# An S4D convolution block with a top-1 mixture of experts: gathers among the experts' work, one load per quarter, drains per expert, a new order

## The chip, the cores and the metric

The kernel runs on one core of a Trainium2 chip. The metric is the device time of one execution in microseconds; the number compared is the median of several timed runs. Besides these there is one profiled execution, from which all rows below come. The core has five engines with a queue each: TensorE (PE; its weight loads are shown as PEld), VectorE (DVE), ScalarE (ACT), GpSimd (POOL), and SyncE (SP), which mostly issues DMAs. ScalarE and GpSimd issue DMAs too.

## The reference

Input `u` is 2048 rows of 512 channels, there are 8 experts with a hidden size of 1792.

```python
# A: S4D convolution over the sequence, N=128 states per channel
dt = exp(log_dt); A = -exp(log_A_real) + 1j * A_imag; C = (C_real + 1j * C_imag) * dt[:, None]
P = exp((A * dt[:, None])[:, :, None] * pos)
K = 2.0 * einsum("dn,dnl->dl", C, P).real
y = irfft(rfft(u_t, 2 * L) * rfft(K, 2 * L), 2 * L)[:, :, :L]   # causal convolution
A_out = y^T + u * D_skip
# B: one expert for each row
gates = softmax(xt @ wg); expert = argmax(gates)
B_out = g * gelu(xt @ w1[expert]) @ w2[expert]                  # g: the normalized gate, 1 for one expert
# whole
h  = x + A(layernorm(x))
h2 = h + B(layernorm(h))
```

The kernel computes every expert for up to a fixed number of rows (288 for the fullest, 232 for the emptiest, `CAPS`), in three parts of up to 96 rows, and treats rows beyond that in a loop at the end which runs as often as there are such rows.

## The kernel before

**Front.** Up to about 310 us the kernel normalizes `u`, transforms it (`u_s1`, `u_ev1`, `u_s2`, `u_ev2`, `spread` copies into `uw`), stores it to a scratch in HBM (`ud`), and builds the convolution's spectra from the state-space parameters (`t_...`). Then the convolution is made for four blocks of 128 channels (`conv`): a block has eight parts `rc`, each of which is loaded, transformed (`c_s2`), multiplied with the spectrum (`c_z`), transformed back in a first step (`c_ia`, L785 and L786), copied from PSUM to a tile `ys` (`c_ys`, L790) and stored to the scratch `yd` (`c_yst`, L793). Once the eight parts of a block are in `yd`, four quarters `q` of it are loaded in another arrangement (`c_y1`, L810) and go through the second step (`c_ib`, L838); the residual is added and the result `h` stored as `hd` in HBM (`r_st`, `r_hd`, L1058). `h` is transposed on PE, copied to tiles `ht` (`r_ev`, L1047) and multiplied with the gate weights (`r_lg`, L1054).

`ys` and `ht` share one pool tag with two buffers. For the last block the tiles of the quarters lie where the experts' weights will be, and each quarter is loaded in four pieces: rows up to 96 of 128 when the first six parts are stored (`c_y3`, two DMAs on SP), the remaining 32 after all eight (`c_y3s` on SP, `c_y3a` on ScalarE's queue).

**Routing.** From the logits VectorE finds each row's expert, its place among that expert's rows, and lists of row numbers: `gi0` for expert 0 and then `gi` for the others. The gate factors are written to HBM as a column `cwd` (`cw_scratch` in the profile).

**Experts.** For each expert `e` and part `k`, GpSimd gathers rows of `h` with their mean and deviation by an indirect DMA (`m_ga`, tile `rows`, 96x516) and the gate factors of these rows with another (`m_gc`, tile `cwt`, 96x1; L1305 is the helper's line for both). VectorE normalizes them, PE transposes, and each float32 matmul is made from three products of high and low parts (`xh`, `xl`; `h`, `l` of the weights: L1400 to L1402, L1423 to L1425). Weights come in slices of 512 KB by SP (`m_w1` in tiles `r1`, `m_w2` in tiles `r2`); ScalarE makes their high part (`m_h`, L1387), VectorE their low part (`m_l`, L1391). At the expert's end VectorE forms gate factor times result plus residual (`m_o`, tile `ot`, L1440) and GpSimd scatters it to the output by an indirect DMA (`m_sc`, L1298). `m_dr` is a drain on GpSimd's queue (L1458), once, behind all 24 scatters. `o_a` and the following prepare the loop over the remaining rows.

**What sets the order.** No task is issued where it is written. `at(t, engine, us, function, ...)` registers it with what it reads and writes; `_Plan.order` then places the tasks one after the other: on each engine, of those that can start within 0.1 us of the earliest, the one with the lowest number in the table `PRI` goes first. `ON` says for tasks that ScalarE or VectorE can do (engine "AV") which does each instance (A or V); where it has a dot the planner takes the one that can start first. `SW` is a penalty for a ScalarE task that needs another activation table. Planned durations are in the `at` calls; a DMA's result counts as there 0.9 us (SP) or 2.2 us (GpSimd) after the issue ends. Buffers are planned as rings (`RINGS`): a tile waits until the users of its slot are placed. The engines then run their queues in this order, held only by semaphores.

Of the kernel before, what the change touches and what calls it, by code (L numbers as in the profile page):

```python
# [22 lines left out]
KR = 3  # L23
# [4 lines left out]
YS = 96  # L28
# [4 lines left out]
def _constants():  # L33
# [11 lines left out]
    co, si = co.transpose(2, 1, 0) / L, si.transpose(2, 1, 0) / L  # L45
# [40 lines left out]
def _dram(ap, dims, off=0):  # L86
# [11 lines left out]
SW = 0  # L98
ON = {
    'p_ev': 'AAAA',  # L100
    'u_norm': 'VVVVAVAAVAVVVVVV',
    'u_ev1': 'AAAAAAAAAAAAAAVAVAAVVVVAAVAVAAVA',
    'u_ev2': 'AAAAAAAAAAAAAAAAVVVVVVVAAAAAAVAA',
    't_vc': 'AAAAAAVAAVAAAAAA',
    't_kt': 'AAAAVAAAAAAAAAAA',
    'c_ev1': 'AAAAAAAAAAAAAAVVAAAAAAVAAAVAAAAA',
    'c_ys': 'AVAAAAAAAAAVAAAAAAAAAAAAAAAAVVVA',
    'c_out': 'AAAAAAAA',
    'r_ev': 'AAAAAAAAAAVAAAAA',
    'r_cb': 'V',  # L110
    'r_c8': 'A',
    'm_xh': 'AAV',
    'm_gh': 'VVA',
}
PRI = {
    'l_wg': [19.9],
    'r_sw': [35.7],
    'r_swe': [43],
    'l_dt': [2],
    'l_x': [16.5, 3.4, 11.7, 6.8],  # L120
    'l_raw': [2.6, 10.9, 15.8, 10.2],
    'l_s1': [15.1],
    'l_m2': [25.5],
    'l_rest': [22.5],
    'p_dt': [3.7],
    'p_exp': [5.7],
    'p_scale': [6.8, 15.8, 21.4, 26.1],
    'p_tr': [7.9, 17.8, 22.4, 27.2],
    'p_ev': [9.6, 20.1, 29.7, 44.6],
    'u_stats': [22.1, 7.8, 16.6, 11.8],  # L130
    'u_mean': [29.4, 16.9],
    'u_dev': [31.7, 20.6],
    'u_var': [32.7, 21.6],
    'u_std': [34.4, 28.3],
    'u_rstd': [35, 28.8],
    'u_norm': [42, 43.1, 39, 37, 41.5, 38, 43, 39.9, 41, 38.4, 40, 36, 29.7, 30.7, 33.4, 32.4],
# [8 lines left out]
    'u_st': [70.1, 74.4, 78.7, 83, 89.1, 93.4, 97.7, 101.9, 112.4, 117.1, 121.4, 125.7, 131.1, 135.4, 139.7, 143.9],  # L145
    'open_main': [147.2],
    'm_load': [151.4],
    't_ep': [13.5, 56.6, 121.3, 185],
    't_r6': [25, 48.2, 117.9, 178.8],
    't_f6': [26.9, 52, 121.8, 180.7],  # L150
    't_trig6': [35.9, 101.5, 172.8, 256.2],
    't_q': [45.3, 107.4, 175.5, 259.8],
    't_qn': [49.9, 115.2, 178.2, 263.2],
    't_vl': [50.9, 53.2, 55.3, 116, 119.2, 123, 179.6, 181.9, 186.5, 264.8, 267.8, 271.1],
    't_r': [21.4, 30.2, 28.5, 22.8, 33.8, 30.8, 32.6, 29.1, 31.4, 32, 33.2, 104.5, 99.1, 97.9, 125.7, 103.9, 123.4, 124.5, 100.3, 100.9,
        99.7, 98.5, 198.8, 199.4, 198.2, 196.4, 192.8, 194.6, 195.8, 194, 193.4, 197.6, 197, 255, 255.6, 252.1, 262, 259.8, 253.2, 262.6,
        252.7, 259.2, 251.4, 253.8],
# [20 lines left out]
    'c_load': [149.9, 181.3, 168.9, 160.1, 148.5, 170.3, 167.4, 178.4, 217, 195.2, 218.5, 235.5, 184.8, 233.3, 223, 190.2, 272, 241,  # L178
# [73 lines left out]
    'o_a': [400],  # L252
    'o_b': [406.6],
    'o_t': [435],
    'o_x': [438.6],
    'o_s': [440.2],
}

# [1393 lines left out]
```

## Time and profile before

| | us |
|---|---|
| timed runs | 820.42, 830.44, 825.66 |
| median of them | 825.66 |
| profiled execution | 817.01 |
| its span on the core | 815.2 |
| last matmul group ends, about | 801.5 |
| last scatter issued | 804.93 to 805.87 |
| first matmul of an expert | 411.7 |
| mean granted clock of TensorE | 0.95 |

Times in the profile count from the span's start. The groups and timelines name an instruction by engine, line, operation, and `out<-in` with the program's tile names; at the end stands how long the engine sat idle before it and what ended that. "issue" means that nothing the profile shows was waited for; "remote" that it was an event that the profile can't assign. POOLq, SPq are the engines' queues. The rows themselves are in the prediction.

### The profile page before, as it was taken

What the parts mean: (1) busy time and instruction counts of PE and PEld (TensorE: products, weight loads), DVE (VectorE), ACT (ScalarE), POOL (GpSimd) and SP (SyncE); (2) the same over time, 40 slices, a digit from 0 to 9 for tenths busy, and PEclk for the clock granted to TensorE, in tenths of its full rate; (3) what the DMA queues carried; (4) which work ended last, traced back from release to release, by engine and by line L of the source; (5) the groups of instructions that cost most, each with busy time, mean ns of one, the idle gap of its engine ahead of it and who ended that gap; (6) DMA issues with size and microseconds to landing.
All of it is one profiled execution on the core that took longest, in us unless ns stands there. A gap on an engine that the chain in (4) does not pass through costs nothing.

```text
span 815.2 us, 19466 instructions
## 1 busy us (share of the span) xinstructions
PE 717.2 (88%) x7752; PEld 671.8 (82%) x7752; DVE 609.6 (75%) x1269; ACT 462.4 (57%) x1024; POOL 79.5 (10%) x77
## 2 busy tenths in 40 slices
PE   2889999898999997987473999999999999999993
PEld 2879989788788787874362999989999999899993
DVE  6999999899999998655834557566666766776752
ACT  6987798558969955112221445545465555546560
POOL 0000000000000000000374003030020303020101
PEclk9999999999999999997585899999999999999997
DMA  9404435975466675798640455655555656566510
GB/s 252 132 1 148 153 93 178 302 197 181 153 209 135 205 183 157 208 290 233 168 134 1 130 177 165 205 161 163 183 176 180 201 189 204 181 194 193 190 68 24
DMA packets 144615, 136.54 MB, mean 167 GB/s; under 512 B 43181, under 2 KB 109361, under 8 KB 144266
## 3 DMA queue, kind: packets, MB, share of 16 engines
q1 hardware_dynamic: 140554, 126.36, 51.7%
q0 software_dynamic: 3776, 8.65, 3.5%
q8 instruction: 62, 1.02, 0.5%
q10 hardware_dynamic: 192, 0.26, 0.1%
q14 instruction: 31, 0.25, 0.1%
HBM read 105.82 MB, written 29.59 MB: 166 GB/s over the span
## 4 chain that ended last, share of the span: by engine, by line
PE 31%; issue 28%; DVE 19%; DMA 8%; ACT 6%; POOL 4%; SPq 2%; ACTq 0%; POOLq 0%; DVEq 0%
DMA yd_scratch<-ys 3%; PE ps_kk L574 3%; PE ps_s L1400 3%; PE ps_s L1402 3%; PE ps_s L1401 3%; DVE rf L662 3%; POOL rows L1305 2%; PE ps_s L555 2%; DVE t L628 2%; PE ps_s L838 2%; PE ps_ga L786 2%; PE ps_ga L785 2%; ACT e L668 2%; DVE xu L547 1%; DVE v L626 1%
## 5 line engine op out<-in xcount | busy, mean ns | idle before, releaser
L1387 ACT CAST h<-r 128x1024 fp32r<-128x1024 f32 x112 | 117.7, 1051 | 100.2 <-PE ps_s L1402 42.2
L1391 DVE TENSOR_TENSOR l<-r,h 128x1024 fp32r<-128x1024 f32 x112 | 136.4, 1222 | 46.9 <-ACT h L1387 43.0
L1400 PE MATMUL ps_s<-xh,h 128*128 128x288 f32 (+5 forms) x448 | 130.6, 292 | 4.4 <-issue 4.1
L1402 PE MATMUL ps_s<-xl,h 128*128 128x288 f32 (+5 forms) x448 | 129.2, 288 | 3.4 <-issue 2.4
L1401 PE MATMUL ps_s<-xh,l 128*128 128x288 f32 (+5 forms) x448 | 129.0, 288 | 2.7 <-issue 2.7
L1405 ACT ACTIVATE g<-ps_s 128x288 f32<-128x288 f32 (+5 forms) x112 | 43.8, 391 | 85.4 <-PE ps_s L1402 67.8
L1400 PEld LDWEIGHTS ps_s<-xh,h 128*128 128x128 f32 x448 | 86.0, 192 | 5.6 <-issue 5.0
L1402 PEld LDWEIGHTS ps_s<-xl,h 128*128 128x128 f32 x448 | 85.6, 191 | 3.7 <-issue 2.2
L1401 PEld LDWEIGHTS ps_s<-xh,l 128*128 128x128 f32 x448 | 85.7, 191 | 3.6 <-issue 3.6
L1425 PE MATMUL ps_kk<-gl,h 128*128 128x288 f32 (+5 forms) x224 | 65.0, 290 | 6.5 <-DVE gl L1412 3.5
L1412 DVE TENSOR_TENSOR gl<-g,gh 128x288 fp32r<-128x288 f32 (+5 forms) x112 | 46.8, 431 | 29.7 <-ACT gh L1408 24.5
L1423 PE MATMUL ps_ga<-gh,h 128*128 128x288 f32 (+5 forms) x224 | 65.0, 290 | 2.2 <-issue 2.2
L1424 PE MATMUL ps_ga<-gh,l 128*128 128x288 f32 (+5 forms) x224 | 64.9, 290 | 2.0 <-issue 2.0
L1423 PE MATMUL ps_kk<-gh,h 128*128 128x288 f32 (+5 forms) x224 | 65.7, 293 | 1.1 <-DVE gh L1408 0.7
L1425 PE MATMUL ps_ga<-gl,h 128*128 128x288 f32 (+5 forms) x224 | 64.9, 290 | 1.7 <-issue 1.7
L1424 PE MATMUL ps_kk<-gh,l 128*128 128x288 f32 (+5 forms) x224 | 64.4, 287 | 0.0
L1298 POOL DMA_INDIRECT out_dram<-ot,si x24 | 26.5, 1105 | 313.2 <-DVE ot L1440 309.8
L785 PE MATMUL ps_ga<-u,mi 128*128 128x128 f32 x256 | 50.5, 279 | 4.1 <-ACT ys L790 3.2
L668 ACT ACTIVATE e<-alp 128x128 f32<-128x128 f32 x256 | 53.5, 316 | 0.1
L997 PE MATMUL ps_pl<-ident 128*128 128x128 f32 x382 | 50.8, 286 | 0.0
L786 PE MATMUL ps_ga<-u,mi 128*128 128x128 f32 x256 | 50.1, 278 | 0.5
L997 PEld LDWEIGHTS ps_pl<-ident 128*128 128x128 f32 x382 | 47.1, 199 | 1.9 <-issue 1.3
(265 smaller groups left out, 1714.2 us busy)
## 6 DMA issues: line engine op xcount, KB each, us to landing
r<-in_B_w_dram SPq DMA_DIRECT2D x112, 512.0 KB
u<-ud_scratch SPq DMA_DIRECT2D x32, 512.0 KB
ud_scratch<-uw SPq DMA_DIRECT2D x16, 512.0 KB
yd_scratch<-ys SPq DMA_DIRECT2D x32, 256.0 KB
y<-yd_scratch SPq DMA_DIRECT2D x24, 256.0 KB
xu<-in_A_u_dram SPq DMA_DIRECT2D x16, 256.0 KB
ud_scratch<-uw SPq DMA_DIRECT2D x16, 256.0 KB
mi<-const_mi_dram SPq DMA_DIRECT2D x1, 3072.0 KB
```

Source lines behind the costliest of these rows:

```text
L668: A.activation(tb[blk, "e"][:, l // 2, :, l % 2], par(alp, blk), AF.Exp, scale=float(l))
L785: T.matmul(pa[:, c], mi[:, 4 * rc + rr, 64:192], z[:, 0, c], start=True, stop=False)
L786: T.matmul(pa[:, c], mi[:, 4 * rc + rr, 0:128], z[:, 1, c], start=False, stop=True)
L997: T.matmul(p, ident, ident, start="pl" not in t_ or "pc" in t_, stop=True, skip_group_check=True)
L1387: A.copy(tile_(("h" + n, e, f), list(r.shape), F32R, pool="wp", name="h" + n, bufs=2), r)
L1391: V.tensor_tensor(tile_(("l" + n, e, f), list(r.shape), F32R, pool="wp", name="l" + n, bufs=2), r, t_["h" + n, e, f].bitcast(F32), op=OP.s ...
L1400: T.matmul(o[:, 0:CAPS[e]], a, xh, start=c == 0, stop=False)
L1401: T.matmul(o[:, 0:CAPS[e]], b, xh, start=False, stop=False)
L1402: T.matmul(o[:, 0:CAPS[e]], a, xl, start=False, stop=c == 3)
L1423: T.matmul(o, a, gh, start=f == 0, stop=False)
L1424: T.matmul(o, b, gh, start=False, stop=False)
L1425: T.matmul(o, a, gl, start=False, stop=f == 13)
```

## The change

The kernel after has the same stages, matmuls and sizes. What differs:

1. `m_gc` of an expert's part now depends on that part's rows gather, `m_ga` is due 32 us ahead of the expert (20 before), and `m_ln`, `m_tr`, `m_xh`, `m_xl` 6 us earlier.
2. `m_dr` is registered once per expert, behind its three scatters.
3. The tiles of `ys` and `ht` are the two halves of one tile `ysr`; the planner says which half (`plan.slot`) and hands the halves out in turn.
4. The constants of the first back-transform are permuted so that a quarter of `yd` can be read with one DMA of 128x2x512; `c_y1` does so for all blocks, for the last one too, and waits for all eight parts. `y1_part`, `y3`, `c_y3`, `c_y3s`, `c_y3a` are gone.
5. `o_a` is cut in three tasks.
6. `PRI` and `ON` hold other values throughout, `SW` goes from 0 to 864.6, and a result counts as there 1.1 us (SP) and 4.0 us (GpSimd) after its issue. With them VectorE does 40 of 64 normalizations of `u` (48 before), 14 of the 32 first and 11 of the 32 second `uw` copies (9 and 8 before), and 2 of the 32 `ys` copies (5 before); ScalarE does the others.

```diff
-    co, si = co.transpose(2, 1, 0) / L, si.transpose(2, 1, 0) / L
+    co, si = (t.reshape(2, 2, 16, 32, 64).transpose(4, 3, 1, 0, 2).reshape(64, 32, 64) / L for t in (co, si))
...
-SW = 0
+SW = 864.6
...
-    'u_norm': 'VVVVAVAAVAVVVVVV',
+    'u_norm': 'V..VAVAAV.AVAVAV',
...
-    'm_gc': [397.2, 396, 398.4],
+    'm_gc': [423.2, 447.8, 473.8],
...
-            end[i] = free[eng] + {"S": 0.9, "G": 2.2}.get(eng, 0.0)
+            end[i] = free[eng] + {"S": 1.1, "G": 4.0}.get(eng, 0.0)
...
-                    held[x] = slots[ring[0]].pop(0)
-                    slots[ring[0]].append(users[x])
+                    self.slot[x], held[x] = slots[ring[0]].pop(0)
+                    slots[ring[0]].append((self.slot[x], users[x]))
...
-        ys = cv["ys", blk, rc] = mp.tile([128, 512], F32, name="ys", tag="ys", bufs=2)
+        ys = cv["ys", blk, rc] = env["ysr"][:, plan.slot[f"ys/{8 * blk + rc}"], :]
...
     def c_y1(blk, q):
-        cv["y1", blk, q] = mp.tile([128, 2, 512], F32, name="y1")
-        for h in range(2):
-            y1_part(nc.sync, blk, q, h, 0, 128)
...
+        if blk < 3:
+            t = cv["y1", blk, q] = mp.tile([128, 2, 512], F32, name="y1")
+        else:
+            t = cv["y1", blk, q] = env["wp"].tile([128, 2, 512], F32, name="y3", tag=("h2", "l2")[q // 2], bufs=2)
+        nc.sync.dma_start(t, _dram(yd, [[32 * 128, 128], [16 * 128, 2], [1, 512]], (blk * 32 * 128 + 4 * q) * 128))
...
-                at(t - 5, "S", 1.2, c_y3, q, r=["h3/0/o"] + [f"yd{n}/{rc}" for rc in range(YS // 16)], w=[f"{ys[q]}/0"])
-                for i, (eng, fn) in enumerate((("S", c_y3s), ("A", c_y3a))):
-                    at(t + 0.01 * q, eng, 0.6, fn, q, r=[f"yd{n}/{rc}" for rc in range(YS // 16, 8)], w=[f"{ys[q]}/{i + 1}", f"yl/0/{q}{i}"])
+                at(t + 0.01 * q, "S", 1.46, c_y1, blk, q, r=["h3/0/o", f"yd{n}"], w=[ys[q], f"yl/0/{q}"])
...
+        env["ysr"] = mp.tile([128, 2, 512], F32, name="ys")
...
-                at(t - 20, "G", 1.2, m_ga, e, k, r=["ix/0" if e else "ix0/0", "hd/0", "xp/0", "wu/0"], w=[f"rows/{e}/{k}"])
-                at(t, "G", 1.2, m_gc, e, k, r=["ix/0" if e else "ix0/0", "cwd/0", "xp/0"], w=[f"cwt/{e}/{k}"])
+                at(t - 32 * (e > 0), "G", 1.2, m_ga, e, k, r=["ix/0" if e else "ix0/0", "hd/0", "xp/0", "wu/0"], w=[f"rows/{e}/{k}"])
+                at(t, "G", 1.2, m_gc, e, k, r=["ix/0" if e else "ix0/0", "cwd/0", "xp/0", f"rows/{e}/{k}"], w=[f"cwt/{e}/{k}"])
...
-        at(KN["rt"] + 8 * 49 + 60, "G", 2.5, m_dr, r=[f"out/{j}" for j in range(NT)])
+            at(t + 58, "G", 2.5, m_dr, e, r=[f"out/{e * KR + k}" for k in range(KR)])
```

**GpSimd's queue.** It stood before, from the first rows gather to the second expert's scatters (`x8` is eight alike in a row; tile numbers tell buffers apart; `gi0` is expert 0's list):

```order
L1305 DMA rows_4780<-hd_scratch,r_gi0_4775 96x516 x3
L1305 DMA rows_4831<-hd_scratch,r_gi_4821 96x516
L1305 DMA cwt_4847<-cw_scratch,r_gi0_4775 96x1 x3
L1305 DMA rows_4831<-hd_scratch,r_gi_4821 96x516 x2
L1305 DMA cwt_4847<-cw_scratch,r_gi_4821 96x1 x8
L1305 DMA cwt_4847<-cw_scratch,r_gi_4821 80x1
...
L1305 DMA cwt_4847<-cw_scratch,r_gi_4821 40x1
L1298 DMA out_0_dram<-ot_5624,si_4892 2048x512
L1298 DMA out_0_dram<-ot_5631,si_4892 2048x512
L1298 DMA out_0_dram<-ot_5664,si_4892 2048x512
L1305 DMA rows_5690<-hd_scratch,r_gi_4821 96x516 x3
```

and stands now:

```order
L1302 DMA rows_4708<-hd_scratch,r_gi0_4705 96x516 x3
L1302 DMA rows_4771<-hd_scratch,r_gi_4757 96x516
L1302 DMA cwt_4790<-cw_scratch,r_gi0_4705 96x1
L1302 DMA rows_4771<-hd_scratch,r_gi_4757 96x516 x2
L1302 DMA cwt_4790<-cw_scratch,r_gi0_4705 96x1
L1302 DMA cwt_4790<-cw_scratch,r_gi_4757 96x1
L1302 DMA cwt_4790<-cw_scratch,r_gi0_4705 96x1
L1302 DMA cwt_4790<-cw_scratch,r_gi_4757 96x1 x2
L1295 DMA out_0_dram<-ot_5520,si_4793 2048x512
...
L1302 DMA rows_5618<-hd_scratch,r_gi_4757 96x516 x3
L1302 DMA cwt_4790<-cw_scratch,r_gi_4757 96x1 x3
```

The 21 one-column gathers that followed the second and third rows gather of expert 1 are now five there and three behind every later expert's rows gathers; a drain, which these rows don't list, stands between the rows gathers and the one-column gathers. At the queue's end the order is three scatters of expert 6, drain, three of expert 7, drain.

**SP's queue** at the end of the last block's convolution, before (`y3` are the quarters' tiles of that block, `h3` is the residual, `xr` holds an earlier block's result on its way to `hd`):

```order
L793 DMA yd_scratch<-ys_4497 128x4x128
L803 DMA h3_4326<-in_A_u_dram 32x64x32
L793 DMA yd_scratch<-ys_4504 128x4x128
L810 DMA y3_4531<-yd_scratch 96x1x512 x2
L810 DMA y3_4546<-yd_scratch 96x1x512 x2
...
L810 DMA y3_4554<-yd_scratch 96x1x512 x2
L1058 DMA hd_scratch<-xr_3801 128x4x128
L1379 DMA r1_4594<-in_B_w1_dram 128x4x256
L1379 DMA r1_4614<-in_B_w1_dram 128x4x256
L1379 DMA r1_4638<-in_B_w1_dram 128x4x256
```

and now:

```order
L805 DMA yd_scratch<-ys_1856 128x4x128
L1050 DMA hd_scratch<-xr_3902 128x4x128
L815 DMA h3_4324<-in_A_u_dram 32x64x32
L826 DMA y3_4477<-yd_scratch 128x2x512
L826 DMA y3_4488<-yd_scratch 128x2x512
L826 DMA y3_4495<-yd_scratch 128x2x512
L826 DMA y3_4503<-yd_scratch 128x2x512
L1050 DMA hd_scratch<-xr_3902 128x4x128
L1050 DMA hd_scratch<-xr_3777 128x4x128
L1380 DMA r2_4538<-in_B_w2_dram 128x2x512
L1376 DMA r1_4551<-in_B_w1_dram 128x4x256
```

Twelve loads became four, all behind the last store; the first weights follow sooner, and a slice of the second matrix (`r2`) comes first.

**ScalarE's queue** at the last copies of `h` for the gate, before:

```order
L1047 COPY ht_4624<-ps_ga_4609 128x512
L1387 CAST h1_4627<-r1_4594 128x1024
L1047 COPY ht_4648<-ps_ga_4629 128x512
L1387 CAST h1_4652<-r1_4614 128x1024
L1047 COPY ht_4665<-ps_ga_4654 128x512
L1076 ACT_TABLE_LOAD
```

and now (the tile `ys_1856` is `ysr`, here as `ht`):

```order
L1039 COPY ys_1856<-ps_ga_4479 128x512
L1039 COPY ys_1856<-ps_ga_4510 128x512
L1039 COPY ys_1856<-ps_ga_4544 128x512
L1384 CAST h2_4572<-r2_4538 128x1024
L1068 ACT_TABLE_LOAD
```

The two weight casts that stood between the copies are behind them.

More of the change, by code (lines that the diff above doesn't have):

```diff
@@ L97 @@
 }
-SW = 0
+SW = 864.6
 ON = {
-    'p_ev': 'AAAA',
-    'u_norm': 'VVVVAVAAVAVVVVVV',
[L102 to L110, printed above, removed]
+    'p_ev': 'A..A',
+    'u_norm': 'V..VAVAAV.AVAVAV',
+    'u_ev1': '..A.V.A...A..AA.A.AAAA.AVVVVV.VV',
+    'u_ev2': 'A.AAAV.AAA.AV....V.VVVV...VAA.A.',
+    't_vc': 'VAAVAA.A.VA.V.AA',
+    't_kt': '.AAA..AA..V.AAA.',
+    'c_ev1': 'AA.A..A....A.AAAA.A.AAAV....AV.A',
+    'c_ys': 'A.AAAA.A..A...A...AA....V...A..V',
+    'c_out': '.AA.AAV.',
+    'r_ev': '...AA.A.AAA.AA..',
+    'r_cb': '.',
@@ L111 @@
     'r_c8': 'A',
-    'm_xh': 'AAV',
-    'm_gh': 'VVA',
+    'm_xh': 'V..',
+    'm_gh': 'VV.',
 }
 PRI = {
[L116 to L130, printed above, removed]
@@ L151 @@
[L151 to L157, printed above, removed]
@@ L249 @@
-    'm_ge': [394.4, 395.8, 397.9],
-    'm_gh': [395.7, 396.5, 398.5],
-    'm_gl': [397.3, 398.9, 399.4],
[L252 to L256, printed above, removed]
+    'l_wg': [-2071.5],
+    'r_sw': [370.6],
+    'r_swe': [-6842.1],
+    'l_dt': [-2420.9],
+    'l_x': [-1637.7, -2189.1, -2191.3, -2183],
+    'l_raw': [-2195.5, -1597.5, -2187.4, -2057.2],
+    'l_s1': [-2183],
+    'l_m2': [-1546.1],
+    'l_rest': [-1584.6],
+    'p_dt': [11.5],
+    'p_exp': [-296.9],
@@ new lines @@
+    'p_scale': [3437.3, 4035.9, 4487.5, 3990.9],
+    'p_tr': [56.9, 1115.8, -791.6, -416.3],
+    'p_ev': [-2271.4, 3965.5, -7614.4, -7711.9],
+    'u_stats': [2063.9, 3238.7, 4442.9, 4403.1],
+    'u_mean': [794.7, -357.4],
+    'u_dev': [2865.3, 3334.2],
+    'u_var': [680.6, -791.7],
+    'u_std': [4887.2, -8287.8],
+    'u_rstd': [4957.7, 3876],
+    'u_norm': [-5404.8, -5140.7, -5519.6, -5503.4, -5263.2, -5503.3, -5530.6, -5348.9, -5287.4, -5519.7, -5441.9, -5287.1, 3597, 3587.7,
+        3448.1, 3583.4],
@@ new lines @@
+    'r_cb': [874.8],
+    'r_ld': [-998.3, -1813.7, -5179, -5209.1],
+    'r_st': [362.8, 689.1, 868.2, 1470.9],
+    'r_ag': [4456.2, 4750.8, 5045.7, 4694.5],
+    'r_sd': [4351.2],
+    'r_tk': [5461.2],
+    'r_rs': [5155],
+    'r_vs': [31],
+    'r_a': [5172.6],
+    'r_p1': [1481.5],
+    'r_p1e': [5144.3],
+    'r_p2': [724.6],
+    'r_s1': [5196.7],
+    'r_ex': [4028],
+    'r_s2': [4951.7],
+    'r_cs': [1388.5],
+    'r_k0': [5157.5],
+    'r_c0': [4354.4],
+    'r_B0': [4835.9, 4890.2],
@@ new lines @@
+    'r_t0': [-221.8, 1497.4],
+    'r_i0': [4579.8],
+    'r_c8': [4335.8],
+    'r_rk': [4868.4],
+    'r_c': [4899.7],
+    'r_M': [4877.5],
+    'r_B': [4878, 4859.6],
+    'r_tb': [930, 898],
+    'r_ix': [5054.5],
+    'r_id': [4905.6],
+    'r_pm': [4950],
+    'm_ga': [-1438.7, -1405.4, -1439.9],
+    'm_gc': [423.2, 447.8, 473.8],
+    'm_ln': [578.8, 415.3, 617.6],
+    'm_tr': [-362.7, 535.5, 1223.2],
+    'm_xh': [440.5, 162.8, 552.1],
+    'm_xl': [469.3, 385.3, 441.5],
+    'm_w1': [-36.5, -83.7, -12.8],
@@ L257 @@
+    'm_h': [4335.2, 758, 3737.9, 3087.8, -68.5, 68.9],
+    'm_l': [4950.1, 5787.1, 5176.7, 5145.1, 535.2, 441.8],
+    'm_w2': [-80.6, -157.7, -73.2],
+    'm_hold': [523],
+    'm_g1': [252.3, 372.4, 404],
+    'm_ge': [1000.3, 423.2, -75.6],
+    'm_gh': [497.6, 561.7, 593.3],
+    'm_gl': [442.1, 462.6, 460.5],
+    'o_a': [422.8],
+    'o_a2': [462.9],
+    'o_a3': [447.3],
+    'o_b': [444.2],
+    'o_t': [528],
+    'o_x': [540.7],
+    'o_s': [844.2],
 }
@@ L333, in order @@
         end, free, tab = {}, {"S": 2.0, "A": 1.9, "V": 1.0, "T": 0.5, "G": 0.5}, None
-        slots = {n: [[] for _ in range(b)] for n, b in set(self.rings.values())}
+        slots = {n: [(i, []) for i in range(b)] for n, b in set(self.rings.values())}
         held = {}
@@ L352, in order @@
                     if ring:
-                        before += held[x] if x in held else slots[ring[0]][0]
+                        before += held[x] if x in held else slots[ring[0]][0][1]
                 if all(j in end for j in before):
@@ L1045, in r_ev @@
     def r_ev(ev, blk, b4):
-        t = t_["ht", blk, b4] = env["mp"]().tile([128, 512], F32, name="ht", tag="ys", bufs=2)
+        t = t_["ht", blk, b4] = env["ysr"][:, plan.slot[f"ht/{4 * blk + b4}"], :]
         ev(t, t_["tr", blk, b4])
@@ L1254, in o_a, with o_a2 @@
             V.tensor_tensor(b[:, k:9], a[:, k:9], a[:, 0:9 - k], op=OP.add)
-        obf = ob[:, 1, :]
+    def o_a2():
+        obf = t_["ob"][:, 1, :]
         ng = sm("ng", [128, 32, 8], pool="xp")
```

208 lines of the change are left out of this document (88 added, 120 removed), and 19 rows, old and new, of the table PRI.

## The prediction

> **What bounds the kernel now.** I read the page's first two parts, then the windows, then the timeline where the windows show a hole, then the waits and the end of the chain. The page:
>
> ```profile
> span 815.2 us, 19466 instructions
> PE 717.2 (88%) x7752; PEld 671.8 (82%) x7752; DVE 609.6 (75%) x1269; ACT 462.4 (57%) x1024; POOL 79.5 (10%) x77
> PE   2889999898999997987473999999999999999993
> DVE  6999999899999998655834557566666766776752
> PEclk9999999999999999997585899999999999999997
> ```
>
> A slice is 20.4 us. VectorE is full in slices 2 to 16 and PE in slices 24 to 39; between them, from about 340 to 460 us, neither is, and the granted clock falls. The windows put numbers on it (busy time and instructions of each engine in each stretch, then clock, DMA share and GB/s):
>
> ```profile
> core 0: us, PE busy (x) PEld busy (x) DVE busy (x) ACT busy (x) POOL busy (x), PEclk, DMA share, GB/s
> 20.00:300.00 280.00, 260.57 (x3814) 234.41 (x3813) 272.29 (x543) 225.37 (x598) 0.00 (x0) 0.99 0.54 161
> 340.00:380.00 40.00, 33.16 (x232) 26.20 (x228) 22.27 (x55) 3.52 (x6) 0.00 (x0) 0.91 0.90 254
> 400.00:420.00 20.00, 12.95 (x84) 12.09 (x84) 10.97 (x34) 4.01 (x6) 14.72 (x14) 0.69 0.55 165
> 420.00:440.00 20.00, 7.52 (x36) 6.31 (x37) 7.85 (x32) 0.84 (x2) 15.12 (x17) 0.66 0.11 27
> 440.00:460.00 20.00, 16.22 (x95) 15.98 (x95) 8.93 (x19) 6.55 (x11) 0.78 (x1) 0.67 0.19 54
> 460.00:480.00 20.00, 20.00 (x152) 20.00 (x151) 11.01 (x15) 9.52 (x16) 0.00 (x0) 0.99 0.58 182
> 480.00:500.00 20.00, 20.00 (x158) 19.98 (x157) 15.13 (x31) 11.27 (x19) 4.70 (x4) 1.00 0.51 162
> ```
>
> Up to 300 VectorE works 272.29 of 280 us, so the convolution front goes at VectorE's pace. From 460 on PE is full: 152 matmuls in 20 us, 0.132 us each. From 420 to 440 PE does 36, VectorE and ScalarE work 7.85 and 0.84 us, and DMA moves 27 GB/s. Only GpSimd is busy. The timeline shows with what:
>
> ```profile
> 406.22 0.98 POOL L1305 DMA_INDIRECT rows<-hd_scratch,r_gi  x1 [1.61 <-DVE r_gi L1232]
> 414.60 0.92 POOL L1305 DMA_INDIRECT cwt<-cw_scratch,r_gi  x1 [0.31 <-issue]
> ...
> 439.86 0.92 POOL L1305 DMA_INDIRECT cwt<-cw_scratch,r_gi  x1 [0.30 <-issue]
> ...
> 417.43 0.29 PE L1424 MATMUL ps_kk<-gh,l 128*128 128x288 f32 x1
> 420.21 0.40 PE L1425 MATMUL ps_kk<-gl,h 128*128 128x288 f32 x1 [2.49 <-issue]
> ...
> 444.58 0.40 PE L1401 MATMUL ps_s<-xh,l 128*128 128x288 f32 x1 [1.00 <-issue]
> ...
> 444.79 1.05 ACT L1387 CAST h<-r 128x1024 fp32r<-128x1024 f32 x1 [16.85 <-remote]
> ```
>
> Between 414.60 and 439.86 stand 21 one-column gathers, 1.23 us apart. PE loses its pace at 417.7, after nine transfers that follow each other from 406.22 on, and regains it at 444.6, 4.7 us behind the last start. Its gaps are labelled issue: no operand was late. All engines hang at once and come free at once, so I read one cause: the back-to-back gathers. What it costs by matmul counts: (152-36) x 0.132 = 15.3 us in 420 to 440, (152-95) x 0.132 = 7.5 us in 440 to 460 (where the clock of 0.67 is part of it), and the gap of 2.49, together 25 us.
>
> **The change, part by part.**
>
> *Gathers.* The 24 one-column gathers stay, but each waits for its expert's rows gather, so 18 move behind the scatters of experts 0 to 5. Nothing near 21 in a row is left: six one-column gathers stand among the three rows gathers of expert 1, and later groups are three scatters, three rows gathers, a drain, three one-column gathers. That such groups are harmless is shown only for six:
>
> ```profile
> 494.34 1.19 POOL L1298 DMA_INDIRECT out_dram<-ot,si  x1 [53.57 <-DVE ot L1440]
> ...
> 502.11 0.99 POOL L1305 DMA_INDIRECT rows<-hd_scratch,r_gi  x1 [0.30 <-issue]
> ```
>
> PE is 20.00 of 20 us busy through their first part (480 to 500, above). Gain: at most 25 us, at least 0 if the stall is only dealt out anew. I take 20, nearest to the upper end, because the first group of expert 0 and 1 is still nine GpSimd transfers long and may lose its last two or three microseconds, and because weight casts (the ScalarE row at 444.79) must catch up before PE has its full pace. GpSimd issues the moved gathers about 40 us before the product that needs them, in time in which it idles:
>
> ```profile
> POOL out_dram L1298 <- DVE ot L1440: 309.8, 13, 53.6
> ACT ys L790 <- DMA yd_scratch<-ys: 19.5, 5, 10.3
> ```
>
> 309.8 us over 13 waits is 24 us a wait; without that cover 3 x 1.23 = 3.7 us an expert would come in front of its scatter, which nobody but the end waits for.
>
> By the Trainium skill's page "SBUF — State Buffer", section "Who interferes with whom", only VectorE and GpSimd share a port, and PE and ScalarE never wait for another engine's port; by it GpSimd's descriptor work couldn't stop PE, the gap of 2.49 us would have another cause, and the gain here could be 0. The trace shows PE and ScalarE stopped as long as VectorE, so if the gathers do it, it isn't by that port.
>
> *Drains.* One drain after all scatters becomes eight, one behind each expert.
>
> ```profile
> 804.93 0.94 POOL L1298 DMA_INDIRECT out_dram<-ot,si  x1 [0.31 <-issue]
> ...
> L1458 POOLq DRAIN  x1: 7598/7598/7598, 804.3 to 804.3; - x1
> ```
>
> The drain ends at 804.3 + 7.6 = 811.9, which is 6.0 us behind the last scatter (805.87), with the span's end behind it. It follows 73 GpSimd transfers. If its length goes with what was issued since the drain before it, the last one now covers three and 6 us fall to under 1; if it is a fixed wait, nothing is won. 0 to -6; I take -4, nearer to the proportional end, because the one measured drain stands behind 73 transfers and the one at the end will stand behind three. The seven others cost at most 7.6 us each, inside the 24 us above; only the gathers and scatters behind them are delayed, and none of these is needed within 20 us. Were that cover gone, the next expert's scatter would be late, and PE still not.
>
> *Loads of y.* 40 loads become 16, of the same bytes. For the last block 12 on SP's queue and 4 on ScalarE's become 4, each behind all eight stores:
>
> ```profile
> 367.61 10.23 SPq L810 DMA_DIRECT2D y<-yd_scratch  x12
> 384.41 1.05 ACT L1387 CAST h<-r 128x1024 fp32r<-128x1024 f32 x1 [1.80 <-DMA r<-in_B_w_dram]
> ...
> 385.84 1.05 ACT L1387 CAST h<-r 128x1024 fp32r<-128x1024 f32 x1
> 386.79 0.59 ACT L1047 COPY ht<-ps_ga 128x512 f32<-128x512 f32 x1
> 386.00 3.59 PE ps_pl L1054 x16
> ```
>
> Issuing takes 10.23 us for 12, so four take about 3.4; SP's stores of h and the weight loads behind them start up to 6.8 us sooner. But 2 MB at the 254 GB/s of this stretch are 8 us of transfer whatever the count, and the queue of parts started before the last store was through, so on the path I count 1. Two weight casts (1.05 each) that ScalarE ran between the last copies of h are now behind them: 2.1, on the path, since the gating matmuls at 386.00 wait for these copies. Together -3; bounds 0 (bandwidth sets it and the casts come back as lateness for PE) and -6.
>
> *Ring.* One tile with two slots in turn in place of two rotating buffers: a copy waits, as before, for the store two places back, so the 19.5 us of waits above stay. Cost 0; a loss only if both slots counted as one, which they don't: each copy's semaphore wait names the store two places back in both programs.
>
> *New order and engine choices.* VectorE gives up 8 normalizations and 3 ys copies and takes 8 uw copies:
>
> ```profile
> L547 DVE TENSOR_SCALAR xu<-xu,mr 128x128 f32<-128x128 f32 x48 | 12.7, 354 | 0.0
> L559 DVE COPY uw<-ps_s 128x512 f32<-128x512 f32 x9 | 6.4, 723 | 0.0
> L581 DVE COPY uw<-ps_kk 128x512 f32<-128x512 f32 x8 | 5.4, 688 | 1.1 <-PE ps_kk L574 1.1
> L790 DVE COPY ys<-ps_ga 128x512 f32<-128x512 f32 x5 | 3.4, 689 | 3.6 <-DMA yd_scratch<-ys 3.6
> ```
>
> That is -8 x 0.354 + 5 x 0.723 + 3 x 0.688 - 3 x 0.689 = +0.8 us; the other swaps are single copies of the same size and cancel to within 2 us. In a front that VectorE paces this is nothing. What the new order can win there is VectorE's idle time, 280 - 272.3 = 7.7 us; what it can lose has no row, and I take the same size: 0, between -8 and +8. The overflow bookkeeping in three pieces is the same work, on an engine that is busy 11 to 15 of 20 us from 460 to 500.
>
> *Sum.* -20 - 4 - 3 + 0 = -27. The profiled execution took 817.0 us (815.2 of span and 1.8 around it), so 790. It was faster than all three timed runs (median 825.66); by 825.66/817.01 = 1.011 the median should be 798.
>
> **The rivals.**
>
> (a) *A smaller stall stays at the start.* For it: nine transfers from the first rows gather of expert 1 to its sixth one-column gather, about as many as stood before 417.7. The last of them plus the 4.7 us of recovery and some half clock leave 12 of the 25 lost: 817 - 13 - 7 = 797, as a median 806.
>
> (b) *The stall isn't the gathers' doing, or each gather carries its own price wherever it stands* (18 us over 21 gathers, 0.9 each). For it: the label issue, and the port rule's silence on PE. Against it: three one-column gathers from 407.50 on didn't slow PE at 412 to 417. Only drain and loads count: 817 - 7 = 810, median 819, within 1%.
>
> (c) *Slower: the stall comes back with every expert.* Place: the groups of three scatters, three rows gathers and three one-column gathers. If the backlog counts across the drain, the ninth transfer falls where PE lost its pace above, and each group stalls PE for 1.2 + 4.7 = 6 us; seven times 42, against 20 saved: 817 + 42 - 27 = 832, median 841. It decides from eight or nine transfers without a pause of several microseconds. Against it: the drain stands just there, and six did nothing.
>
> (d) *The front slips.* VectorE idles where the new order waits for PE or a store; from 27 us on the gain is gone, from 35 on it is slower, 825 to 835. Against it: equal work on each engine.
>
> **How the numbers follow.** Forecast 0.64, (a) 0.13, (b) 0.10, (c) 0.07, (d) 0.06. The forecast's own range, from the bounds (stall -25 to -15, drain -6 to 0, loads -6 to 0, front -8 to +8, not all at one end) is 782 to 812. With (a) and (b) the range becomes 782 to 819, and (c), (d) and some tails are left out, under 0.2. This kernel's runs scatter by about 1%, so a change below that can't be told from none: faster by over 1% is the forecast and (a), 0.77; within 1% (b) and a little of (d), 0.12; slower (c) and the rest of (d), 0.11.
>
> **What would show it.** In the changed profile: PE at 150 matmuls or so in each 20 us from about 415 on and no row with issue gaps of over a microsecond (gathers right); last drain under 2 us (drain right); four y loads in under 4 us and gating logits about 3 us sooner (loads right); VectorE 270 or more of 280 busy up to 300 (front right). The prediction is wrong if gaps labelled issue stand behind each expert's scatters, if the last drain still takes 6 us and PE still halts after the routing, or if the last stage of the front ends over 10 us later.

## The result, and the profile after

| | before | after | |
|---|---|---|---|
| median of the timed runs, us | 824.37 (820.42 to 830.44, 4 runs) | 782.54 (780.66 to 785.81, 4 runs) | ratio 0.949, interval 0.942 to 0.956 |
| profiled execution, its span, us | 815.2 | 780.4 | -34.8 |
| first matmul of expert 0 | 411.7 | 408.9 | -2.8 |
| from there to the first of expert 1 | 74.0 | 45.8 | -28.2 |
| from there to the end of the last expert matmul | 314.5 | 314.9 | +0.4 |
| from there to the span's end | 15.0 | 10.8 | -4.2 |

The median of before is now of four runs; the table ahead of the prediction had three. The lower rows are places in the two timelines: the starts of the first L1400 (now L1397) matmul of an expert, and the end of the last matmul of the second product. Nearly all of the difference lies in expert 0 and behind the last matmul. The windows of the kernel after, with the columns of before:

```profile
core 0: us, PE busy (x) PEld busy (x) DVE busy (x) ACT busy (x) POOL busy (x), PEclk, DMA share, GB/s
20.00:300.00 280.00, 257.58 (x3806) 235.59 (x3806) 273.96 (x543) 221.33 (x585) 0.00 (x0) 0.98 0.55 161
340.00:380.00 40.00, 35.39 (x226) 28.35 (x227) 19.27 (x51) 6.28 (x11) 0.00 (x0) 0.83 1.02 286
400.00:420.00 20.00, 17.00 (x104) 16.33 (x103) 12.48 (x36) 5.27 (x10) 11.81 (x11) 0.68 0.53 166
420.00:440.00 20.00, 18.71 (x144) 18.48 (x143) 19.00 (x45) 11.09 (x20) 0.00 (x0) 1.00 0.52 159
440.00:460.00 20.00, 20.00 (x153) 20.00 (x152) 10.64 (x14) 10.44 (x17) 0.00 (x0) 1.00 0.59 174
```

Where PE did 36 and 95 matmuls in two stretches of 20 us, it now does 144 and 153, at full clock, and GpSimd does nothing there. The front is as full as it was: VectorE 273.96 of 280 us. What GpSimd's timeline and PE's show from expert 1's gathers on:

```profile
404.94 0.92 POOL L1302 DMA_INDIRECT rows<-hd_scratch,r_gi  x1 [2.07 <-DVE hn L1338]
...
415.87 1.02 POOL L1302 DMA_INDIRECT cwt<-cw_scratch,r_gi  x1 [0.31 <-issue]
...
474.84 0.92 POOL L1302 DMA_INDIRECT rows<-hd_scratch,r_gi  x1 [0.30 <-issue]
479.88 0.92 POOL L1302 DMA_INDIRECT cwt<-cw_scratch,r_gi  x1 [4.12 <-issue]
...
424.09 0.40 PE L1398 MATMUL ps_s<-xh,l 128*128 128x288 f32 x1 [1.29 <-DVE l L1388]
```

Nine transfers follow each other from 404.94 to 415.87, and PE has one gap, which isn't issue but a weight's low part. The 4.12 us ahead of a one-column gather is a drain: it parts the group of nine into six and three. The drains, and the last scatter:

```profile
L1455 POOLq DRAIN  x8: 3391/9056/10195, 469.2 to 773.7; - x8
...
774.32 0.94 POOL L1295 DMA_INDIRECT out_dram<-ot,si  x1 [0.30 <-issue]
```

The columns are the shortest, median and longest length in ns, and the first and last start. The last drain, the shortest, ends 777.1, 1.8 us behind the last scatter; before it was 6.0.

### The profile page after: what moved, and what is told of

Its sections match the earlier page's. It is cut to its first block, busy times and chain, and to the rows that moved or that the text cites. A ratio compares the mean times of both kernels' runs of the same rounds, so it can differ in the third digit from the quotient of the medians.

```text
span 780.4 us, 19458 instructions
## 1 busy us (share of the span) xinstructions
PE 712.0 (91%) x7760; PEld 672.8 (86%) x7760; DVE 611.6 (78%) x1268; ACT 461.2 (59%) x1025; POOL 83.6 (11%) x77
## 4 chain that ended last, share of the span: by engine, by line
issue 31%; DVE 21%; PE 18%; ACT 10%; DMA 9%; POOL 6%; SPq 2%; POOLq 1%; ACTq 0%; DVEq 0%
POOL cwt L1302 2%; DVE t L640 2%; DMA yd_scratch<-ys 2%; ACT rf L669 2%; POOL out_dram L1295 2%; ACT e L680 2%; DMA y<-yd_scratch 2%; DVE v L638 2%; PE ps_kk L586 2%; DMA xr<-in_A_u_dram 2%; PE ps_s L1398 2%; PE ps_s L1399 1%; PE ps_s L1397 1%; POOL rows L1302 1%; PE ps_s L831 1%
## 5 line engine op out<-in xcount | busy, mean ns | idle before, releaser
L1397 PE MATMUL ps_s<-xh,h 128*128 128x288 f32 (+5 forms) x448 | 129.8, 290 | 0.0
L1397 PEld LDWEIGHTS ps_s<-xh,h 128*128 128x128 f32 x448 | 85.3, 190 | 0.3
L989 PEld LDWEIGHTS ps_pl<-ident 128*128 128x128 f32 x390 | 48.9, 204 | 2.0 <-issue 1.7
```

Of the source, the lines that this page charges most:

```text
L989: T.matmul(p, ident, ident, start="pl" not in t_ or "pc" in t_, stop=True, skip_group_check=True)
L1397: T.matmul(o[:, 0:CAPS[e]], a, xh, start=c == 0, stop=False)
```

## The experiments

Each series of runs was on one chip, with the kernel before timed beside it. That mattered as much as the largest edit: the kernel before took 820 and 822 us in two series (chips 14 and 1) and 800 in two others (chips 4 and 8).

### The kernel before again, and each side of the gathers alone (chip 4, before 800.63)

The first run is the unchanged kernel.

> The kernel before, unchanged, for a second profile. In the first profile expert 0 took from 411.7 to 485.7 us (74.0) with PE stopped for issue between 417.7 and 444.6, and the execution was 817.0 where the timed runs were 820 to 830. If the length of the stall is what varies between executions, expert 0 takes another length here, say 70 to 85 us, and the span moves with it, all else within 1 us. If it is fixed, expert 0 takes 74 again and the difference to the timed runs lies in another stage.

Measured: 800.86 us; expert 0 from 416.7 to 468.0, 51.3 us. Its windows:

```profile
400.00:420.00 20.00, 11.87 (x79) 11.06 (x80) 15.14 (x44) 3.33 (x5) 10.51 (x10) 0.56 0.50 146
420.00:440.00 20.00, 18.95 (x141) 18.48 (x140) 16.44 (x49) 7.98 (x14) 16.04 (x14) 0.96 0.37 106
440.00:460.00 20.00, 20.00 (x147) 20.00 (x147) 11.47 (x17) 9.04 (x14) 9.34 (x8) 0.96 0.50 144
```

GpSimd issues the same long row (16.04 of 20 us busy), and PE does 141 matmuls beside it. On this chip there is no stall. Neither expectation had that.

The second run gives the kernel before the spread alone.

```diff
-                at(t, "G", 1.2, m_gc, e, k, r=["ix/0" if e else "ix0/0", "cwd/0", "xp/0"], w=[f"cwt/{e}/{k}"])
+                at(t, "G", 1.2, m_gc, e, k, r=["ix/0" if e else "ix0/0", "cwd/0", "xp/0", f"rows/{e}/{k}"], w=[f"cwt/{e}/{k}"])
```

> The kernel before with one edit: an expert's one-column gather waits for its rows gather, so 18 of them leave the long row. Front and routing keep their order word for word. Theory: the long row of gathers stops all engines, expert 0 falls from 74 to about 46 us, the span from 815 to about 787, ratio about 0.966. Rival: the gain at expert 0 came from the new order of the casts and weights, and the spread alone gives nothing: expert 0 stays at 70 or more, ratio 0.99 to 1.00.

801.72 us, ratio 1.003 (1.000 to 1.006). Without a stall, the spread gives nothing. (The groups of three scatters, three rows gathers and three one-column gathers, here without a drain in them, leave no gap labelled issue on PE either.) The third run is the mirror image, the kernel after with this line as it was.

> The kernel after with one edit undone: the one-column gathers don't wait for the rows, so 21 of them stand in a row again behind the second rows gather of expert 1. Theory: the stall is back, issue gaps on PE between about 416 and 443, expert 0 about 74 us, span about 808. Rival (the new order does it): no gaps, expert 0 about 46, span 780 to 784.

778.47 us, ratio 0.974 (0.969 to 0.978), expert 0 in 44.1 us, no issue gap. Both looked like the rival, but the chip couldn't tell the theories apart, since no stall was there to come or go. What the run does show is that on this chip the rest of the change is worth 22 us. (The kernel after itself was not run on chip 4 or 8.)

The fourth run keeps the long row of the kernel before and puts drains into it.

```diff
-        gather(tile_("cwt", [PR, NT], name="cwt")[0:n, j:j + 1], index(e, k), cwd)
+        gather(tile_("cwt", [PR, NT], name="cwt")[0:n, j:j + 1], index(e, k), cwd); (G.drain() if j % 3 == 2 else None)
```

> The kernel before with its long row of one-column gathers kept, but with a drain on GpSimd's queue behind every third of them (seven within the row). Theory A (a backlog of descriptors behind GpSimd does it, a drain waits it out): the row becomes longer, some 3 x 1.2 + 3.4 = 7 us for three gathers, and PE has no issue gaps over 1 us; expert 0 near 46 us, span near 790. Theory B (each gather beyond the first nine costs its share, whatever stands between): expert 0 stays at 70 or more.

806.83 us, ratio 1.009 (1.007 to 1.012): slower, expert 0 in 60.3 us, and nothing learnt of the stall. One of the drains stands ahead of two rows gathers of expert 1, and those have readers. Rows of GpSimd, VectorE and PE, in this order:

```profile
413.87 0.92 POOL L1305 DMA_INDIRECT cwt<-cw_scratch,r_gi  x1 [0.30 <-issue]
420.57 1.14 POOL L1305 DMA_INDIRECT rows<-hd_scratch,r_gi  x1 [5.77 <-issue]
...
427.70 0.54 DVE L1341 TENSOR_SCALAR hn<-rows 96x512 f32<-96x512 f32 x1 [2.42 <-DMA rows<-hd_scratch,r_gi]
...
436.00 0.61 PE L1401 MATMUL ps_s<-xh,l 128*128 128x288 f32 x1 [4.54 <-DVE l L1391]
```

The rows come 5.5 us later, VectorE waits for them, and what is queued behind on VectorE, a weight's low part, stops PE for 4.5 us. A drain is free only where no one waits for what stands behind it.

### The row and the drains where the stall exists (chip 14, before 820.12)

The kernel after, unchanged:

> The kernel after, unchanged, beside the kernel before on the same chip. In the runs so far the kernel before took 820 to 830 us with the stall at expert 0, and 796 to 805 without it (51 us for expert 0). If the before of this series is near 825: ratio about 0.95, stall absent in after. If it is near 800: the stall isn't there to be removed, and the ratio is that of the rest of the change, about 0.973 as for the kernel after with its gathers in a row; the rival is that spreading still gives something of its own and the ratio is 0.965 or less.

781.96 us, ratio 0.951 (0.944 to 0.958). Beside it, again, the kernel after with the full row:

> The kernel after with its 21 one-column gathers in a row, again, on the same chip as the kernel after. If before is near 825 here, the theory that the row brings the stall expects issue gaps on PE and 805 to 810 us; the rival (the new order keeps PE out of it) expects 780. If before is near 800, both expect the time of the kernel after within 0.5%.

801.89 us, ratio 0.976 (0.968 to 0.984): 19.9 us more than the kernel after on the same chip. The stall is back, in the new order too:

```profile
400.00:420.00 20.00, 16.39 (x109) 15.46 (x110) 12.66 (x36) 3.54 (x6) 14.27 (x14) 0.74 0.55 166
420.00:440.00 20.00, 6.76 (x23) 4.62 (x22) 4.71 (x21) 1.79 (x3) 15.12 (x17) 0.60 0.10 27
440.00:460.00 20.00, 17.36 (x111) 16.86 (x112) 14.10 (x26) 11.30 (x20) 0.78 (x1) 0.80 0.36 110
```

PE's timeline of this run, the first and the last of its 18 gaps labelled issue:

```profile
419.01 0.39 PE L1421 MATMUL ps_kk<-gh,l 128*128 128x288 f32 x1 [0.35 <-issue]
...
444.44 0.40 PE L1399 MATMUL ps_s<-xl,h 128*128 128x288 f32 x1 [0.30 <-issue]
```

So on this chip the row brings the stall in the new order, and the kernel before, which has the row, shows it in the old one. Taking the row out of the old order alone was tried only on chip 4, where there was no stall to take away.

The two runs compared differ in one thing more. One and the same source was built into two slightly different programs: this run's kernel is that of the third run on chip 4 to the letter, yet VectorE and ScalarE have another number of instructions (the busy line of the page, chip 4 first):

```profile
PE 710.5 (91%) x7760; PEld 671.5 (86%) x7760; DVE 612.4 (79%) x1268; ACT 461.8 (59%) x1025; POOL 89.6 (12%) x77
PE 717.0 (90%) x7760; PEld 676.1 (84%) x7760; DVE 611.4 (76%) x1267; ACT 461.8 (58%) x1026; POOL 80.9 (10%) x77
```

Between 510 and 551 us their instructions also stand in another order. On these two engines the kernel after, in both its profiles, is built as the one on chip 4. Here the difference is small beside the row: this run takes 18.0 us more than the kernel after in expert 0, and within 0.6 us of it in experts 1 to 3 and in experts 4 to 6.

Then the drains. The kernel before with a drain per expert, registered as in the change:

```diff
-        at(KN["rt"] + 8 * 49 + 60, "G", 2.5, m_dr, r=[f"out/{j}" for j in range(NT)])
+            at(t + 58, "G", 2.5, m_dr, e, r=[f"out/{e * KR + k}" for k in range(KR)])
```

> The kernel before with one edit: a drain behind each expert's three scatters in place of one behind all. If a drain's length goes with the transfers since the drain before, the last one falls from 7.6 to about 3.4 us and the time by 4 us (ratio 0.995). If it is a fixed wait behind the last scatter, it stays at 6 us behind the last scatter and the ratio is 1.000. The seven others should show no gap on PE.

822.51 us, ratio 1.001 (0.997 to 1.006): no gain. The drain itself did what was expected of it, 3.1 us at the end in place of 7.6, and the span ends 4.8 us behind the last scatter in place of 9.3. No gap labelled issue stands behind the seven others. But VectorE's order is another from expert 1 on, and experts 5 and 6 took 45.5 and 46.6 us in place of 44.3 and 42.4, with PE waiting for low parts. How much of that is the order's isn't shown: the unchanged kernel took 46.1 and 44.7 there on chip 4. The kernel after with one drain at the end:

```diff
-            at(t + 58, "G", 2.5, m_dr, e, r=[f"out/{e * KR + k}" for k in range(KR)])
+        at(KN["rt"] + 8 * 49 + 60, "G", 2.5, m_dr, r=[f"out/{j}" for j in range(NT)])
```

> The kernel after with one edit undone: one drain behind all scatters. If a drain's length goes with what was issued since the last, it is 7.6 us again, ends 6 us behind the last scatter, and the time rises by 4 us against the kernel after. If the drains only matter by their number, the time falls by the seven drains that are gone, or stays.

794.69 us, 12 to 13 more than the kernel after, three times what a drain at the end can do: from the last scatter's end to the span's end it is 9.4 us in place of 5.1, and PE ends at 774.8 in place of 770.1. Experts 4 to 6 take 134.9 us in place of 127.3. VectorE's and ScalarE's order differs, too, from that of the kernel after.

### Seven drains left out, a shorter row, drains in the row (chip 1, before 821.81)

```diff
     def m_dr(e):
-        G.drain()
+        G.drain() if e == 7 else None
```

> The kernel after with its plan unchanged and seven of the eight drains left out: only the one behind the last expert's scatters stays. The one-drain kernel before this one also had another order at the last experts, and lost 12.7 us. If a drain's length goes with what was issued since the last drain, the time from the last scatter's end to the span's end is 9.4 us in place of 5.1 and the time about 786 (4 more than the kernel after); PE ends at the same place, about 770. If the seven drains also hold back something else that matters, PE ends elsewhere than 767 to 771.

793.19 us, ratio 0.966 (0.962 to 0.971); the kernel after had 0.951 on chip 14. The tail is as expected: the one drain takes 7.6 us, and from the last scatter's end (782.2) to the span's end (791.6) are 9.4 us. But PE ends at 776.6, not at 770, and experts 4 to 6 take 134.9 us in place of 127.3. GpSimd's and PE's rows at expert 5:

```profile
663.23 0.92 POOL L1302 DMA_INDIRECT cwt<-cw_scratch,r_gi  x1 [0.30 <-issue]
665.68 1.08 POOL L1302 DMA_INDIRECT cwt<-cw_scratch,r_gi  x1 [0.30 <-issue]
...
666.53 0.28 PE L1399 MATMUL ps_s<-xl,h 128*128 128x256 f32 x1 [0.50 <-issue]
667.95 0.28 PE L1398 MATMUL ps_s<-xh,l 128*128 128x256 f32 x1 [1.02 <-issue]
670.69 0.38 PE L1422 MATMUL ps_kk<-gl,h 128*128 128x256 f32 x1 [1.41 <-DVE gl L1409]
```

and GpSimd's at the same place of the unchanged kernel, where PE has no gap:

```profile
661.93 0.88 POOL L1302 DMA_INDIRECT rows<-hd_scratch,r_gi  x1 [0.30 <-issue]
668.10 0.92 POOL L1302 DMA_INDIRECT cwt<-cw_scratch,r_gi  x1 [5.29 <-issue]
```

Without the drain the group of nine runs through, and PE stops for issue at its end, with a low part late behind it. With the drain it pauses 5.3 us, and nothing stops.

The program that ran was not the kernel after with drains left out, though, as the expectation has it. The busy lines of the one-drain kernel on chip 14 and of this one:

```profile
PE 709.5 (90%) x7760; PEld 669.1 (85%) x7760; DVE 611.3 (77%) x1267; ACT 460.8 (58%) x1026; POOL 82.8 (10%) x77
PE 716.2 (90%) x7760; PEld 675.6 (85%) x7760; DVE 611.6 (77%) x1267; ACT 461.3 (58%) x1026; POOL 82.6 (10%) x77
```

On VectorE, ScalarE and GpSimd the two ran the same instructions in the same order, that of the full-row run on chip 14. PE's order differs at one place, at the start of expert 4. So they are nearly one experiment on two chips, with the same 134.9 us in experts 4 to 6 both times. The order isn't what costs this: the full-row run on chip 14 has it too, with groups of six and a drain in each, and takes 127.9 us there without a gap labelled issue. The drains between the groups thus keep off a loss of 7 us that the gathers moved behind the scatters would bring; the drain at the end is worth 4.3.

The second run on this chip frees the one-column gathers of experts 0 to 3, so that 11 stand in a row and 15 transfers follow each other from 404.50 to 422.99 (the expectation counted one too many).

```diff
-... r=["ix/0" if e else "ix0/0", "cwd/0", "xp/0", f"rows/{e}/{k}"], w=[f"cwt/{e}/{k}"])
+... r=["ix/0" if e else "ix0/0", "cwd/0", "xp/0", f"rows/{e if e > 3 else 0}/{k}"], w=[f"cwt/{e}/{k}"])
```

> The kernel after with the one-column gathers of experts 0 to 3 freed: 11 stand in a row behind the third rows gather of expert 1, 16 GpSimd transfers without a pause in all (12 in the kernel after with none of the stall, 27 in the kernel with the full row, which lost 19 us). If the stall, on a chip that shows it, begins at a fixed count of about ten and lasts until some 4 us behind the last, it runs from about 418 to 428 here and costs 6 to 8 us: expert 0 at 52 to 54 us. If it needs a long row, expert 0 takes 45 to 49. On a chip without the stall both give 780.

786.60 us, ratio 0.961 (0.955 to 0.967), expert 0 in 50.9 us. PE's gaps begin about 419 and are over at 426:

```profile
419.49 0.24 PE L1344 MATMUL ps_pl<-ident,hn 96*128 96x96 f32 x1 [0.30 <-issue]
...
425.85 0.40 PE L1422 MATMUL ps_kk<-gl,h 128*128 128x288 f32 x1 [1.00 <-issue]
```

Expert 0 lies between the two forecasts, 5.1 us above the 45.8 of the run that follows, on the same chip. So the price grows with the row: nothing at nine transfers (the kernel after), 5 us at 15, 20 at 27 (the full row on chip 14). Here PE's gaps begin about the twelfth.

The third run has the full row, with drains in it.

```diff
-... r=["ix/0" if e else "ix0/0", "cwd/0", "xp/0", f"rows/{e}/{k}"], w=[f"cwt/{e}/{k}"])
+... r=["ix/0" if e else "ix0/0", "cwd/0", "xp/0"], w=[f"cwt/{e}/{k}"])
...
-        gather(tile_("cwt", [PR, NT], name="cwt")[0:n, j:j + 1], index(e, k), cwd)
+        gather(tile_("cwt", [PR, NT], name="cwt")[0:n, j:j + 1], index(e, k), cwd); (G.drain() if j % 3 == 2 else None)
```

> The kernel after with the full row of 21 one-column gathers and a drain behind every third. On a chip that shows the stall: theory A (it is work that GpSimd has handed out and that is not finished; a drain waits it out) expects no issue gaps of over 1 us on PE and expert 0 at 46 to 50 us; theory B (every gather beyond the first ten costs its microsecond) expects expert 0 at 66 or more, as with the row alone. On a chip without it both give 780 to 783.

781.55 us, ratio 0.951 (0.946 to 0.956), expert 0 in 45.8 us, the time of the kernel after:

```profile
400.00:420.00 20.00, 16.77 (x101) 16.10 (x100) 12.16 (x36) 5.85 (x10) 10.70 (x11) 0.68 0.56 166
420.00:440.00 20.00, 18.83 (x145) 18.59 (x144) 19.03 (x44) 10.60 (x20) 10.66 (x7) 1.00 0.52 159
440.00:460.00 20.00, 20.00 (x152) 20.00 (x152) 10.63 (x14) 10.09 (x16) 9.18 (x9) 1.00 0.56 170
```

PE is full, though all one-column gathers still stand in one row. GpSimd's first, one behind a drain, and the last:

```profile
405.98 0.92 POOL L1302 DMA_INDIRECT cwt<-cw_scratch,r_gi  x1 [0.30 <-issue]
...
430.45 1.89 POOL L1302 DMA_INDIRECT cwt<-cw_scratch,r_gi  x1 [3.88 <-issue]
...
465.44 0.92 POOL L1302 DMA_INDIRECT cwt<-cw_scratch,r_gi  x1 [0.30 <-issue]
```

So the gathers' number alone isn't what stops the engines, and theory B is out. Theory A fits, but one rival is left: with the drains the row takes 60 us in place of 33, and in 420 to 440 GpSimd issues 7 gathers in place of 17. Whether it is the drain's waiting that helps or only the slower pace was not tried; that needs a row with pauses and no drains.

### The GpSimd part alone on the old order (chip 8, before 799.99)

The spread of the second run, and drains where the kernel after has them, written so that the plan doesn't change:

```diff
-        gather(rows(e)[0:n, k, :], index(e, k))
+        gather(rows(e)[0:n, k, :], index(e, k)); (G.drain() if e > 1 and k == 2 else None)
...
-        scatter_out(t_["ot", e, k][0:n], t_["si", e][0:n, k:k + 1])
+        (G.drain() if e == 7 and k == 0 else None); scatter_out(t_["ot", e, k][0:n], t_["si", e][0:n, k:k + 1])
```

> The kernel before in its old order, engine choices and loads, with the GpSimd part of the change alone: one-column gathers behind their rows gathers, and drains at the places where the kernel after has them. The question is what the new order and the loads are worth, a term that the prediction put at 0 and 3. On a chip that shows the stall (before near 820, kernel after 782): if they are worth nothing, this kernel takes 782; if they gave what is missing beside 20 for the row and 4.3 for the last drain, it takes about 796, with expert 0 at 51 us as in the runs of the old order without the stall (46 in the new). On a chip without it (before near 800): 796 by the last drain alone, ratio 0.995.

796.51 us, ratio 0.996 (0.994 to 0.999): 3.5 us, about the last drain. The new order and the loads are worth the rest: 0.996 here against 0.974 for the new order with the full row on chip 4, both beside a before of 800, is 18 us. From first to last expert matmul the old order takes 368.5 us in this profile and the new one 355.5 in that of chip 4. Two places of the old order:

```profile
432.36 1.85 PE L1284 MATMUL ps_pl<-r_a,r_B 128*128 128x21 f32 x15 [0.48 <-DVE r_B L1279]
...
720.01 0.57 PE L1425 MATMUL ps_kk<-gl,h 128*128 128x240 f32 x1 [2.37 <-DVE gl L1412]
```

The 32 matmuls of the overflow bookkeeping (L1284; this row ends with its window, at 15) stand inside expert 0 and take 3.8 us there; the new order does them at expert 2 in 3.6 us, which moves time and saves none. Expert 2 gets 1.0 us longer and expert 0 7.8 shorter. And PE waits for low parts of the activations (gl) at experts 5 and 6, which take 2.2 and 3.7 us less in the new order. From first to last expert matmul PE sits idle 8.4 us in this profile and 1.1 in that of chip 4; that is 7.3 of the 13 us, and the other 6 aren't accounted for.

## Why the prediction was right, and where it was off

The direction, the place and the main mechanism were right; the time, 782.54 against 798 (782 to 819), lies half a microsecond inside the range's lower end. The sum said 27 us less, the medians fell by 41.8; that the time is inside is partly luck, since the largest part of what was missing, the new order, stood in the sum with 0. Term by term:

- **The row of gathers, -20.** Measured 19.9 on chip 14, by the kernel after with and without the row. The cause is shown by three edits: the row brings the stall back in the new order, a shorter row brings a shorter one, and drains in the row take it away. In the first pair expert 0 fell by 28.2, the row's 20 and some 8 more; the new order makes expert 0 shorter by 7.8 without a stall, too. What the prediction couldn't see from one trace is the condition: on chip 4 the same program has no stall, and the term is 0 (ratio 1.003 for the spread alone). Rival (b), that the gathers aren't the cause, is thus wrong where there is a stall. Where there is none it is right that they cost nothing, but not that little is gained: the rest of the change is worth 22 us on chip 4.
- **The last drain, -4.** Measured 4.2 between the last matmul and the span's end in the first pair, 4.3 with only the inner drains left out. "Goes with what was issued since the drain before" holds in its direction: 7.6 us behind all 73 transfers, 5.0 behind 42 (the run with drains in the old row), 3.1 to 3.4 behind three. It isn't in proportion, and the sign "last drain under 2 us" failed: it took 3.4 us, ending 1.8 behind the last scatter, where the step had hoped for under 1.
- **The seven other drains, 0.** Right against the kernel before, whose groups of six had no drain and leave no gap labelled issue either. The step said that the drains are hidden in GpSimd's idle time, which is so; it didn't say what they are for. Rival (c) had that: without the drain, groups of nine do stop PE where the stall exists. It happens at experts 4 to 6, not at all seven, and costs 7 us, not 42. What the rival named as evidence against itself, that the drain stands just there, is what decided.
- **Loads of y and casts, -3.** Four loads are issued in 2.8 us in place of 10.2 for twelve, as said; the last gating logits start 1.5 us sooner, not 3. The first expert matmul came 2.8 us earlier in the first pair, but among the profiles of the old order it lies anywhere from 411.7 to 416.7, so the term isn't shown. Which of the two would have done it was not tried.
- **The new order, 0 between -8 and +8.** Mis-sized. The front stayed as it was, as said. But the step looked at the front alone, and most of the order's gain of some 13 to 18 us lies in the experts: about half of it is PE's waits, for low parts above all, and the rest is not taken apart. In the first pair's profiles the gain is seen in expert 0 alone, and experts 1 to 7 take as long as before. The profiled execution of before had 1.7 and 1.5 us of PE's gaps in experts 5 and 6, that of the same kernel on chip 4 1.9 and 2.5. Whether such waits make its timed runs longer isn't shown.
- **The factor 1.011 to the median.** Wrong. It took the gap between the profiled execution and the timed runs as common to both kernels. The gap belonged to the kernel before, whose executions scatter from 816 to 830 where the stall exists; those of the kernel after lie within 6 us in each series, and its profiled one is among them. Without the factor the sum of -27 gives 790.

Together on chip 14: 820.1 - 782.0 = 38.1, of which 19.9 are the row and 4.3 the last drain; the remaining 14 are left for the order and the loads. They are a remainder and weren't measured by themselves there; the 18 us without a stall are a second estimate, between two series.

The Trainium skill's page "SBUF — State Buffer", section "Who interferes with whom", says that PE and ScalarE never wait for anyone. By that rule the row couldn't stop PE. The runs on chips 14 and 1 disagree: 23 matmuls in 20 us beside the row and 145 beside the same row with drains. On chip 4, with 141 beside the row, they agree. The measurement decides: where the stall exists, the row stops PE and ScalarE, and whatever does it isn't a port of that table.

## What to carry to other kernels

When all engines crawl at once and only one issues, look at that one's queue: a long row of GpSimd DMAs without a pause could stop the whole core here, and spreading them or draining between small groups took that away. A drain costs nothing if nothing behind it is awaited while it lasts (3 to 14 us in these runs), and costs PE's time if a gather with a reader stands behind it. Time an edit beside the old kernel on the same chip, and on more than one chip: the largest term here was 20 us on one chip and nothing on another. And where an order is planned, see from the traces that the two kernels compared differ only in what was edited: two different edits ran in the same order here, and one source in two.

## What the runs showed of the hardware that was not expected

- The stall comes with the series: present on chips 14 and 1, absent on 4 and, by the times alone, on 8, with the same kernel, in all timed runs of a series (816 to 830 against 796 to 805). Each chip had one series, so whether it is the chip or something else of the series stays open.
- In the stall nothing that the profile shows is saturated: from 420 to 440 DMA is busy 0.10 to 0.11 and moves 27 GB/s, the granted clock is 0.60 to 0.66 with PE mostly idle, and many of PE's instructions start one by one, 0.7 us or a multiple of it apart. SP hangs as well: in the full row it issues one slice of weights in these 20 us on chip 14 and seven on chip 4. What resource it is stays open; gathers of another width in such a row weren't tried.
- When no drain stands in it, the group of nine is nearly harmless at experts 1 to 3 (0.5 to 0.7 us of gaps on chips 1 and 14) and not at 4 to 6. It may depend on how much was issued since the last drain, but that was only seen, not tested.
- A drain behind all 73 transfers takes 7.6 us although GpSimd had been idle for 26 us ahead of the last three; in the run with drains in the old row, where 42 transfers follow the drain before it, the last one takes 5.0:

```profile
L1458 POOLq DRAIN  x1: 5041/5041/5041, 796.7 to 796.7; - x1
```
